# Conversions of weights spread differently over the attention, and the output weights of the first layer split two steps ahead

## The chip, the cores and the metric

The kernel runs on one core of a Trainium2 chip. The metric is the device time of one execution in microseconds (us), as the median of several runs. TensorE (PE) multiplies, VectorE (DVE), ScalarE (ACT) and GpSimd (POOL) work element by element, SyncE (SP) issues most of the transfers. Each engine takes its instructions in the order in which the program has them.

## The reference

Attention with a sigmoid in place of the softmax, then two dense layers with different activations; everything in float32.

```python
# q, k, v: (4 batches, 12 heads, 448 rows, 64)
scores = q @ k.T / sqrt(64) - log(448)
x = sigmoid(scores) @ v              # reordered to (1792, 768)
h = x @ w_in1;  x = silu(h) @ w_out1                  # 768 -> 2048 -> 768
h = x @ w_in2
g = (a0 + a1*h + a2*h**2 + a3*h**3) / (1 + |b0|*|h| + |b1|*h**2 + 1e-6)
out = g @ w_out2
```

The inputs q, k, v arrive as float32; the four weight matrices arrive as float64 bit patterns, that is as pairs of 32-bit words.

## The kernel before

**Precision.** TensorE multiplies in a format of fewer bits (fp32r). Each operand is split into a rounded high part (a copy on ACT) and a remainder (a subtraction on DVE, or on POOL in layer 2); a product is three matmuls: high by high, high by low, low by high.

**Conversions.** There are 64 weight tiles of 128x768: 16 of W_in and 16 of W_out for each of the two layers. `conv()` (L159 to L178) turns one from float64 bits into float32: one ACT instruction (L169, absolute value) and four DVE instructions (L170 to L175) on a tile that a transfer of 768 KB has put into one of two stage buffers (`stg`). `conv_outs()` then lets SP store the result (384 KB, to `w0i`, `w0o`, `w1i` or `w1o` in DRAM) and behind it load the float64 tile that is two conversions further on, into the stage buffer just read. So a conversion waits for the load that the conversion two before it has issued.

**Attention.** A loop over n = 0 to 47 (`for n in range(2 * NPT)`), two iterations for each pair of heads, four for each two pairs. An iteration issues: score matmuls of one or two units (`attn_QK`, L298, into `pair` tiles of PSUM, of which there are three), in odd iterations the transposes of a later pair of heads (`attn_T`, L272 and L275, into a `pair` tile too), the sigmoid of each unit (`attn_S`, ACT, L313, which frees the `pair` tile), the products with V of the units of the iteration before (`attn_AV`, L322, into `hb0` for even pairs of heads and `hb1` for odd ones), in every fourth iteration (n = 0, 4, ..., 44) the copies `attn_E` of both finished `hb` tiles out of PSUM (DVE, L335 or L338), then the split of the transposed tile (`attn_C`, ACT L281, DVE L283). From n = 21 on operands of layer 1 are made beside this; at n = 40 SP loads four tiles `wf` of converted W_in (L495), and at n = 43 ACT begins to split them (L355, and sums on DVE). Last in an iteration stands `conv()`, in those that the tuple `CONVS` lists; its store and the next load follow at the beginning of the next iteration. `CONVS` holds 19 iterations here: 2, the pairs (4, 5), (8, 9) to (24, 25), and 29, 33, 37, 42, 44, 46.

**Layer 1, first half.** x @ w_in1 in 16 groups (p1 to p7, seven block products for eight); 13 of the groups hold one conversion each. After `silu` the tiles `gd` go to DRAM.

**Layer 1, second half.** `second(n)` for n = 0 to 63 (L610 to L620): 18 matmuls with one tile pair `woH`, `woL` (split from `wos`, which ACT loads, L598) and one tile `gx` (split from `f`, which ACT loads from `gd`, L583). The order of the steps around n = 2, with the last pieces of the first half (`c21`, `both`, `c12`), is written out by hand. In loop n the split of the W_out tile is that of n + 1, the split of `gd` that of n + 2; the load of W_out n + 5 stands right behind the split that frees its buffer. The remaining conversions are spread by `conv_by(n)`: one in four steps up to n = 16, then evenly up to n = 52. Behind every 16 steps `results1` copies six results out of PSUM.

**Layer 2** follows with its own splits on POOL; the change does not touch it.

Of the kernel before, what the change touches and what calls it, by code (L numbers as in the profile page):

```python
# [41 lines left out]
def attention_moe_moe(ctx: ExitStack, tc: tile.TileContext, q, k, v, w_in1, w_out1, w_in2, w_out2, a, b2, out):  # L42
# [10 lines left out]
    KF = DFF // P  # L53
# [65 lines left out]
    def coefficients_abs():  # L119
        nc.scalar.activation(absb, ab[:, 4:6], AF.Abs)  # L120
# [223 lines left out]
    def split(src, x, eng=None):  # L344
        nc.scalar.copy(x[:, 0, :], src)
        (eng or nc.vector).tensor_tensor(out=x[:, 1, :], in0=src, in1=x[:, 0, :].bitcast(F32), op=ALU.subtract)

    def split2(src, h, lo, eng=None):
        nc.scalar.copy(h, src)  # L349
        (eng or nc.vector).tensor_tensor(out=lo, in0=src, in1=h.bitcast(F32), op=ALU.subtract)  # L350
# [148 lines left out]
    def silu(t, src, g, hi_f, second):  # L499
        nc.scalar.activation(t, src, AF.Silu)  # L500
        nc.sync.dma_start(out=gd[g % HF + hi_f * HF][2 * (g // HF) + second], in_=t)
        f448.put(t)
# [61 lines left out]
    def c12(g):  # L564
        silu(sums[g, "r"], sums[g, "r"], g, 0, 1)

    def c21(g):
        silu(f448.get(), bank("a", g), g, 1, 0)
# [16 lines left out]
    def split_gd(n):  # L585
        if n < B * KF:
            t = gq.pop(n)
            gx[n] = hl.get()
            split(t, gx[n])
            f448.put(t)  # L590
# [4 lines left out]
    def load_wo1(c):  # L595
        if c < KF:
            wo_in[c] = wos.get()
            nc.scalar.dma_start(out=wo_in[c], in_=wd[0][c]["o"])  # L598

    def split_wo1(c):  # L600
        if c < KF:
            t = wo_in.pop(c)
            split2(t, woH[c], woL[c])
            wos.put(t)
# [200 lines left out]
    with tc.manual_schedule():  # L805
# [24 lines left out]

        first_ops = operands0()
        NOPS = 7 * HK
        CONVS = (2, *(n for n in range(4, 28) if n % 4 < 2), 29, 33, 37, 42, 44, 46)
        waiting = []
        for n in range(2 * NPT):
            e, part = n // 4 * 2, n % 4
# [47 lines left out]
            if n == 12:  # L884
                coefficients_abs()
            if n in CONVS:
                conv()
# [136 lines left out]
        split_gd(2)  # L1024
        load_g(4)
        load_g(5)
        split_gd(3)
        NL1 = B * KF
        more = x_all.rearrange("p a b -> p (a b)").bitcast(I32).rearrange("p (e t) -> p e t", t=2)
        stage.put(more)  # L1030
# [8 lines left out]
        for n in range(2, NL1):  # L1039
            load_g(n + 4)  # L1040
            second(n)
            split_gd(n + 2)
            if n + 1 < KF:
                split_wo1(n + 1)
                load_wo1(n + 5)
            if n == 2:
                c21(last)
                both(last, "r", "c")
                c12(last)
            if n == KF - 1:  # L1050
                wos_s.close()
                l2_p = ctx.enter_context(tc.tile_pool(name="l2a", bufs=1, side="right", reuse_waits="tile"))
                hx.put(*fixed("hx", KD, [P, 2, BK], F32R, l2_p))
                wi_f.extend(fixed("wif", 4, [P, DM], F32, l2_p))
            if n % KF == KF - 1:
                results1(n // KF)
            conv_to(conv_by(n))
            m = n - (NL1 - KF)
            if m == 4:
                assert done["conv"] == len(order)  # L1060
            if m == 1:
                whr.put(w0[:2], w0[2:])
                for c in range(4):
                    load_w2("i", c)
            if m == 5:
                for d in range(HK):
                    load_x(0, d)
            if 7 <= m < 7 + KD:
                split_x(0, m - 7)
                if m - 7 < HK:  # L1070
                    load_x(0, m - 7 + HK)
            if m in (KF - 6, KF - 4):
                split_w("i", (m - KF + 6) // 2)
# [67 lines left out]
```

## Time and profile before

| | us |
|---|---|
| median of 3 runs | 1088.09 (1085.32 to 1091.08) |
| the profiled execution | 1086.84 |
| its span, first to last instruction | 1085.0 |
| PE busy | 1072.8 (99%) |
| DVE busy | 867.4 (80%) |
| ACT busy | 620.5 (57%) |
| POOL busy | 343.0 (32%) |

The attention runs from the beginning to 171.7 us, the first half of layer 1 to about 383, its second half to about 612, layer 2 to the end. The granted clock of TensorE is 0.999 on average. PE is the engine with the least idle time, so the time changes by what PE waits, and a change on another engine counts where PE comes to wait for it or no longer does. A matmul of 448 columns starts 0.20 us after the one before it when nothing holds it, although each is listed as 0.36 long: matmuls overlap, so what a stall costs is read from one start to the next.

### The profile page before, as it was taken

The page shows a single profiled execution, that of the slowest core. Times are in us where ns is not written, and L with a number is a line of the kernel's source. Part 1 is how long each engine was busy: PE and PEld are TensorE (multiplying, and loading weights), DVE is VectorE, ACT ScalarE, POOL GpSimd, SP SyncE. Part 2 cuts the span into 40 slices and gives each one's busy share as a digit, 9 for nine tenths or more (in the row PEclk, how much of TensorE's full clock was granted, in tenths as well). Part 3 has the DMA queues.
Part 4 walks back from the last instruction along what each step waited for, and adds up shares of the span by engine and source line. Part 5 has one row for each costly group of instructions (what it writes and reads, how often), then busy time and mean ns, then how long its engine had stood idle before and what let it go on. Part 6 is the DMA issues. An engine that isn't in the chain of part 4 may idle for free.

```text
span 1085.0 us, 15860 instructions
## 1 busy us (share of the span) xinstructions
PE 1072.8 (99%) x5822; PEld 913.9 (84%) x5822; DVE 867.4 (80%) x1030; ACT 620.5 (57%) x1023; POOL 343.0 (32%) x246
## 2 busy tenths in 40 slices
PE   9999999999999999999999999999999999999997
PEld 6555557999999988999999888889999888889997
DVE  4779877888977656887974397888999988888996
ACT  6678886656655534433333265556666655566664
POOL 2122210000000000000001175665777656657774
PEclk9999999999999999999999999999999999999999
DMA  8999877778576866998994470001011100101001
GB/s 211 275 292 269 248 228 245 252 247 275 172 251 221 281 222 218 335 347 303 358 329 160 175 284 1 23 22 50 9 30 31 44 1 1 32 14 59 1 1 44
DMA packets 102685, 177.96 MB, mean 164 GB/s; under 512 B 9168, under 2 KB 76752, under 8 KB 102608
## 3 DMA queue, kind: packets, MB, share of 16 engines
q1 hardware_dynamic: 90320, 155.38, 44.3%
q10 hardware_dynamic: 12224, 21.57, 6.2%
q8 instruction: 46, 0.75, 0.3%
q14 instruction: 31, 0.25, 0.1%
q0 software_dynamic: 64, 0.00, 0.0%
HBM read 123.31 MB, written 53.61 MB: 163 GB/s over the span
## 4 chain that ended last, share of the span: by engine, by line
PE 90%; DMA 3%; DVE 3%; ACT 2%; issue 1%; ACTq 1%; SPq 0%; POOL 0%; DVEq 0%; POOLq 0%
PE acc L748 14%; PE acc L481 13%; PE acc L751 7%; PE hb L677 7%; PE hb L678 7%; PE hb L679 7%; PE hb L481 5%; PE hb L322 5%; PE pair L298 5%; PE acc L619 5%; PE acc L617 5%; PE acc L618 5%; DMA stg<-in_moe_w_in_dram 2%; PE hb L619 1%; PE hb L617 1%; PE hb L618 1%
## 5 line engine op out<-in xcount | busy, mean ns | idle before, releaser
L350 POOL TENSOR_TENSOR w<-wif,w 128x768 fp32r<-128x768 f32 x33 | 61.2, 1855 | 444.0 <-DMA xio<-xs 438.1
L313 ACT ACTIVATE f<-pair,nls 128x896 f32<-128x896 f32 x84 | 80.6, 1007 | 21.9 <-PE pair L298 21.8
L705 DVE RECIPROCAL stg<-stg 128x512 f32<-128x512 f32 (+1 forms) x28 | 84.9, 3033 | 0.0
L692 ACT ACTIVATE stg<-hb,absb 128x512 f32<-128x512 f32 (+1 forms) x44 | 28.0, 636 | 99.0 <-PE hb L679 98.9
L169 ACT ACTIVATE bits<-stg 128x768 f32<-128x768 f32 x54 | 48.8, 904 | 54.2 <-DMA stg<-in_moe_w_in_dram 23.7
L322 PE MATMUL hb<-f,vs 128*64 128x448 f32 (+1 forms) x384 | 73.9, 554 | 0.0
L481 PE MATMUL acc<-xb,wr 128*128 128x448 f32 x315 | 67.7, 366 | 0.0
L350 POOL TENSOR_TENSOR wh<-wif,wh 128x768 fp32r<-128x768 f32 x31 | 57.3, 1850 | 27.5 <-ACT wh L349 25.6
L481 PEld LDWEIGHTS acc<-xb,wr 128*128 128x128 f32 x315 | 59.1, 188 | 5.3 <-issue 0.7
L748 PE MATMUL acc<-w,hx 128*128 128x512 f32 x174 | 61.4, 393 | 0.0
L618 PE MATMUL acc<-xa_all,woH 128*128 128x448 f32 x168 | 61.4, 365 | 0.0
L619 PE MATMUL acc<-xa_all,woL 128*128 128x448 f32 x168 | 61.4, 365 | 0.0
L617 PE MATMUL acc<-xa_all,woH 128*128 128x448 f32 x168 | 61.3, 365 | 0.0
L350 POOL TENSOR_TENSOR wh<-wof,wh 128x768 fp32r<-128x768 f32 x32 | 59.2, 1849 | 5.1 <-ACT wh L349 4.9
L748 PE MATMUL acc<-wh,hx 128*128 128x512 f32 x171 | 60.3, 393 | 0.0
L350 POOL TENSOR_TENSOR w<-wof,w 128x768 fp32r<-128x768 f32 x32 | 59.2, 1849 | 0.4 <-ACT w L349 0.2
L748 PE MATMUL acc<-wh,hy 128*128 128x512 f32 x165 | 58.9, 398 | 0.4 <-POOL hy L715 0.4
L748 PE MATMUL acc<-w,hy 128*128 128x512 f32 x162 | 57.3, 396 | 0.0
L170 DVE TENSOR_SCALAR bits<-bits 128x768 f32<-128x768 f32 x64 | 38.4, 599 | 21.8 <-ACT bits L169 21.1
L298 PEld LDWEIGHTS pair<-xa_all 64*128 64x128 f32 x384 | 34.3, 188 | 23.8 <-issue 11.3
L172 DVE SCALAR_TENSOR_TENSOR bits<-stg,bits 128x768 int32<-128x768 int32 x54 | 52.5, 972 | 1.9
L175 DVE SCALAR_TENSOR_TENSOR bits<-stg,bits 128x768 int32<-128x768 int32 x54 | 51.7, 958 | 1.9
(237 smaller groups left out, 3297.8 us busy)
## 6 DMA issues: line engine op xcount, KB each, us to landing
stg<-in_moe_w_in_dram SPq DMA_DIRECT2D x27, 768.0 KB, 7.4
stg<-in_moe_w_out_dram SPq DMA_DIRECT2D x27, 768.0 KB, 6.4
gd<-f SPq DMA_DIRECT2D x64, 224.0 KB, 3.2
f<-gd ACTq DMA_DIRECT2D x64, 224.0 KB, 4.8
wf<-w0i SPq DMA_DIRECT2D x32, 384.0 KB, 3.7
w0i<-bits SPq DMA_DIRECT2D x16, 384.0 KB, 4.1
w0o<-bits SPq DMA_DIRECT2D x16, 384.0 KB, 4.2
wos<-w0o ACTq DMA_DIRECT2D x16, 384.0 KB, 4.4
```

The costliest lines, as they stand in the source:

```text
L298: nc.tensor.matmul(p[:, j, :S], K[rows[j], a_, c * P : (c + 1) * P], Q[rows[j], b_, :], start=(n == 0), stop=(n == len(turns) - 1),)
L313: nc.scalar.activation(t, p[:, :, :S], AF.Sigmoid, bias=nls, scale=QKSCALE)
L322: nc.tensor.matmul(hb[i_ % 2][j * D : (j + 1) * D, :S], vs[i_][part, j, c * D : (c + 1) * D], t[part, j], start=(c == 0), stop=(c == LAST),)
L350: (eng or nc.vector).tensor_tensor(out=lo, in0=src, in1=h.bitcast(F32), op=ALU.subtract)
L481: nc.tensor.matmul(o, w_[:, w], x[:, i_, :], start=first and kk == 0 and n_ == 0, stop=kk == HK - 1 and n_ == 2, skip_group_check=not first,)
L617: nc.tensor.matmul(o, woH[c][:, w], x[:, 0, :], start=(c == 0), stop=False)
L618: nc.tensor.matmul(o, woH[c][:, w], x[:, 1, :], start=False, stop=False)
L619: nc.tensor.matmul(o, woL[c][:, w], x[:, 0, :], start=False, stop=(c == KF - 1))
L677: nc.tensor.matmul(o, wh[:, w], x[:, 0, :wd_], start=first, stop=False)
L678: nc.tensor.matmul(o, wh[:, w], x[:, 1, :wd_], start=False, stop=False)
L705: nc.vector.reciprocal(t0, t1)
L748: nc.tensor.matmul(acc[t][:, :BK], a_, w_[:, :BK], start=first, stop=last)
```

## The change

Three edits. The tuple `CONVS` has 18 iterations instead of 19: 10 instead of 13 up to n = 27, and 8 instead of 6 after it, 40, 42, 43, 45 and 46 among them. The 64 conversions stay; as the later ones are counted from what is done, all later conversions move by one place and `conv_by` has one more to spread over n = 17 to 52. `split_gd(3)` moves from ahead of the loop to n = 2. In the loop, W_out is split two steps ahead, its load stands in front of the split and ahead of the split of `gd`, and at n = 2 the last pieces of the first half come before the splits.

```diff
@@ attention
-        CONVS = (2, *(n for n in range(4, 28) if n % 4 < 2), 29, 33, 37, 42, 44, 46)
+        CONVS = (2, 6, 8, 10, 14, 16, 18, 22, 24, 26, 30, 34, 38, 40, 42, 43, 45, 46)
@@ layer 1, second half
         split_gd(2)
         load_g(4)
         load_g(5)
-        split_gd(3)
...
         for n in range(2, NL1):
             load_g(n + 4)
             second(n)
-            split_gd(n + 2)
-            if n + 1 < KF:
-                split_wo1(n + 1)
-                load_wo1(n + 5)
             if n == 2:
                 c21(last)
                 both(last, "r", "c")
                 c12(last)
+                split_wo1(3)
+                split_gd(3)
+            if n + 2 < KF:
+                load_wo1(n + 5)
+                split_wo1(n + 2)
+            split_gd(n + 2)
```

**DVE in iterations 43 and 44 of the attention.** `pair_276` is the last transposed tile, `sf` and `wf` belong to layer 1's weights, `bits` and `stg` to a conversion, `hb_274` and `hb_275` are `hb0` and `hb1`. Before:

```order
173 L283 TENSOR_TENSOR xa_all<-pair_276,xa_all 128x512
174 L283 TENSOR_TENSOR qx<-pair_276,qx 128x448
175 L367 TENSOR_TENSOR sf_246<-wf_1_243 128x384
176 L364 TENSOR_TENSOR sf_246<-sf_246,wf_0_242 128x384
177 L338 COPY xio<-hb_274 128x448
178 L338 COPY xio<-hb_275 128x448
179 L360 TENSOR_TENSOR wr_1850<-wf_0_242,wr_1849 128x768
180 L170 TENSOR_SCALAR bits_66<-bits_66 128x768
```

The same place after the change:

```order
165 L283 TENSOR_TENSOR xa_all<-pair_276,xa_all 128x512
166 L283 TENSOR_TENSOR qx<-pair_276,qx 128x448
167 L367 TENSOR_TENSOR sf_246<-wf_1_243 128x384
168 L364 TENSOR_TENSOR sf_246<-sf_246,wf_0_242 128x384
169 L170 TENSOR_SCALAR bits_64<-bits_64 128x768
170 L171 TENSOR_SCALAR bits_64<-bits_64 128x768
171 L172 SCALAR_TENSOR_TENSOR bits_64<-stg_63,bits_64 128x768
172 L175 SCALAR_TENSOR_TENSOR bits_64<-stg_63,bits_64 128x768
173 L338 COPY xio<-hb_274 128x448
174 L338 COPY xio<-hb_275 128x448
```

The conversion of n = 43 stands in front of the copies out of `hb0` and `hb1`; before, the next conversion came behind them.

**SP at n = 40 and behind it.** `vs` are loads of V, `wf` the loads of layer 1's first weights, `w0i` and `w0o` stores of converted tiles, `stg` loads for conversions, `xs` stores of attention results. Before:

```order
160 L201 DMA vs_1745<-in_v_dram 64x2x256
161 L495 DMA wf_0_242<-w0i_143 128x768
162 L495 DMA wf_1_243<-w0i_159 128x768
163 L495 DMA wf_0_244<-w0i_145 128x768
164 L495 DMA wf_1_245<-w0i_161 128x768
165 L155 DMA w0o_144<-bits_65 128x768
166 L143 DMA stg_62<-in_moe_w_out_dram 128x1536
```

The same place after the change:

```order
154 L201 DMA vs_1745<-in_v_dram 64x2x256
155 L495 DMA wf_0_242<-w0i_143 128x768
156 L495 DMA wf_1_243<-w0i_159 128x768
157 L495 DMA wf_0_244<-w0i_145 128x768
158 L495 DMA wf_1_245<-w0i_161 128x768
159 L155 DMA w0i_171<-bits_65 128x768
160 L139 DMA stg_63<-in_moe_w_in_dram 128x6x256
161 L155 DMA w0i_157<-bits_66 128x768
162 L143 DMA stg_62<-in_moe_w_out_dram 128x1536
```

Row 159 is now the store of the conversion of n = 40 (before, that of n = 42), and row 160 the load into `stg_63`, which the conversion of n = 43 reads.

**ACT in the second half of layer 1.** `wos` are loaded W_out tiles, `woH` their high parts, `f<-gd` loads and `xa` high parts of `gd`. Before, two steps (n = 4 and 5):

```order
432 L583 DMA f<-gd_0_111 128x448
433 L345 CAST xa_215<-f 128x448
434 L349 CAST woH_3702<-wos_3503 128x768
435 L598 DMA wos_3503<-w0o_162 128x768
436 L583 DMA f<-gd_0_115 128x448
437 L345 CAST xa_216<-f 128x448
438 L349 CAST woH_3704<-wos_3504 128x768
439 L598 DMA wos_3504<-w0o_164 128x768
```

After the change, two steps (n = 3 and 4):

```order
428 L583 DMA f<-gd_0_107 128x448
429 L598 DMA wos_3495<-w0o_160 128x768
430 L349 CAST woH_3695<-wos_3496 128x768
431 L345 CAST xa_all<-f 128x448
432 L583 DMA f<-gd_0_111 128x448
433 L598 DMA wos_3496<-w0o_162 128x768
434 L349 CAST woH_3697<-wos_3497 128x768
435 L345 CAST xa_215<-f 128x448
```

Before, the load into a `wos` buffer stands right behind the copy from that buffer; now a whole step lies between the two.

## Rows read from the trace of the kernel before

**Rows 1.** The page: engines over the span, and TensorE's granted clock in 40 slices.

```profile
PE 1072.8 (99%) x5822; PEld 913.9 (84%) x5822; DVE 867.4 (80%) x1030; ACT 620.5 (57%) x1023; POOL 343.0 (32%) x246
...
PEclk9999999999999999999999999999999999999999
```

**Rows 2.** Waits of PE: who waited for whom, total us, times, longest us.

```profile
PE pair L272 <- ACT f L313: 1.7, 3, 0.6
PE hb L619 <- DVE woL L350: 1.7, 2, 1.0
```

**Rows 3.** Timeline of PE, attention, n = 7: start, us, what, idle before.

```profile
32.69 0.78 PE L298 MATMUL pair<-xa_all 64*128 64x448 f32 x6
34.01 0.63 PE L272 MATMUL pair<-ident,km 128*128 128x128 f32 x4 [0.55 <-ACT f L313]
```

**Rows 4.** Timeline of ACT, attention: conversions of n = 5 and 9.

```profile
32.06 0.90 ACT L169 ACTIVATE bits<-stg 128x768 f32<-128x768 f32 x1 [3.48 <-DMA stg<-in_moe_w_in_dram]
...
46.18 0.90 ACT L169 ACTIVATE bits<-stg 128x768 f32<-128x768 f32 x1 [2.55 <-DMA stg<-in_moe_w_in_dram]
```

**Rows 5.** Timeline of SP, attention: the load for the conversion of n = 9.

```profile
37.33 0.39 SPq L139 DMA_DIRECT2D stg<-in_moe_w_in_dram  x1
```

**Rows 6.** Timeline, layer 1, second half, PE and ACT at n = 7 and 11.

```profile
402.01 0.37 PE L618 MATMUL hb<-xa,woH 128*128 128x448 f32 x1
...
403.43 0.47 PE L619 MATMUL hb<-xa,woL 128*128 128x448 f32 x1 [1.05 <-DVE woL L350]
...
404.25 0.57 ACT L345 CAST xa_all<-f 128x448 fp32r<-128x448 f32 x1 [4.27 <-DVE woL L350]
...
417.92 0.36 PE L618 MATMUL hb<-xa_all,woH 128*128 128x448 f32 x1
...
418.89 0.47 PE L619 MATMUL hb<-xa_all,woL 128*128 128x448 f32 x1 [0.61 <-DVE woL L350]
```

**Rows 7.** Timeline of PE: first matmuls of second(2) and second(3).

```profile
383.57 0.36 PE L617 MATMUL hb<-xa_all,woH 128*128 128x448 f32 x1
...
387.22 0.36 PE L617 MATMUL hb<-xa_all,woH 128*128 128x448 f32 x1
```

**Rows 8.** Timeline of ACT in layer 1: results1 at n = 31.

```profile
492.42 0.53 ACT L625 COPY f<-acc 128x448 f32<-128x448 f32 x1 [8.84 <-PE acc L619]
```

**Rows 9.** Timeline of ACT, n = 42 (a conversion) and 43 (split of wf).

```profile
154.90 0.89 ACT L169 ACTIVATE bits<-stg 128x768 f32<-128x768 f32 x1
...
158.60 0.84 ACT L355 CAST wr<-wf 128x768 fp32r<-128x768 f32 x1
```

**Rows 10.** Timeline of DVE, n = 40 to 44.

```profile
149.91 0.62 DVE L364 TENSOR_TENSOR xk<-xk,xk 128x448 f32<-128x448 f32 x1
...
158.00 0.96 DVE L175 SCALAR_TENSOR_TENSOR bits<-stg,bits 128x768 int32<-128x768 int32 x1
...
160.59 0.56 DVE L364 TENSOR_TENSOR sf<-sf,wf 128x384 f32<-128x384 f32 x1
161.68 1.16 DVE L338 COPY xio<-hb 128x448 f32<-128x448 f32 x2 [0.53 <-PE hb L322]
```

**Rows 11.** Timeline of PE, n = 45: second score unit, then the V products.

```profile
162.28 0.78 PE L298 MATMUL pair<-qx,xa_all 64*128 64x448 f32 x6
162.99 1.72 PE L322 MATMUL hb<-f,vs 128*64 128x448 f32 x8
```

**Rows 12.** Timeline of SP: the four loads of wf.

```profile
152.43 2.01 SPq L495 DMA_DIRECT2D wf<-w0i  x4
```

**Rows 13.** DMA issues near 154.1: KB each, median us to landing.

```profile
wf<-w0i SPq DMA_DIRECT2D x1, 384.0 KB, 5.9
```

**Rows 14.** DMA issues, 117 to 119 us: load and store of one conversion.

```profile
stg<-in_moe_w_in_dram SPq DMA_DIRECT2D x1, 768.0 KB, 6.0
w0i<-bits SPq DMA_DIRECT2D x1, 384.0 KB, 2.9
```

**Rows 15.** Timeline of PE: the first score matmuls of the kernel.

```profile
7.37 2.61 PE L298 MATMUL pair<-xa_all 64*128 64x448 f32 x12
```

## The prediction

> **What bounds the kernel now.** I read the page first. PE is busy for 99% of the span and its granted clock stands at 9 tenths or more in every slice [rows 1], so nothing that is merely moved between the other engines changes the time; only a wait of PE does. Next I read the waits of PE. Two groups lie where the change works: three waits in the attention, 1.7 us together, ended by a sigmoid on ACT, and two in the second half of layer 1, 1.7 us together, ended by the split of W_out on DVE [rows 2]. Then I followed each back in the timelines.
>
> In the attention, the six score matmuls of n = 7 that start at 32.69 are done in 0.71, so the transposes were due at 33.40; they start at 34.01 [rows 3]. They wait for the `pair` tile that the sigmoid frees, and ACT was late because it stood for 3.48 in front of the conversion of n = 5, whose stage buffer was still loading; the conversion of n = 9 stands for 2.55 in the same way [rows 4]. The loop behind it: conversion at 32.06, next load into that buffer issued at 37.33, landed for 46.18 [rows 4, 5]. That is 14.1 us, where four iterations of PE without a stall take 13.5 (14.1 less the 0.6 of the stall). Conversions in pairs, two in four iterations, each pair feeding the next, thus lose 0.6 per turn, until the loads become faster.
>
> In layer 1 the second matmul of n = 7 starts at 402.01 and the third, which reads `woL`, at 403.43; at n = 11 the pair is 417.92 and 418.89 [rows 6]. Behind the first of these ACT is idle for 4.27 until DVE has split `woL` [rows 6]: the load that stands right behind the copy on ACT may not overwrite the buffer before DVE has read it, and everything on ACT stands behind that load. Steps with a conversion on top then take longer than the 3.65 us that PE needs (383.57 to 387.22 [rows 7]).
>
> **The change part by part.**
>
> *Attention, first part: gain 1.9.* Ten conversions instead of thirteen. The two stage buffers alternate, so a conversion depends on the one two before it in the list: 6 feeds 10, 8 feeds 14, 10 feeds 16, 14 feeds 18. The distances are now 4, 6, 6 and 4 iterations, and the distance of four is always followed by a longer one, so lateness cannot add up as it does before, where all are four. At a distance of four the load is 0.6 late (14.1 against 13.5). ACT stood 2.55 to 3.48 when PE lost 0.6, so a wait of 0.6 on ACT stays within what PE can bear, 2 us or more. I take all three stalls as gone: 3 x (34.01 - 33.40) = 1.8, with the others read alike 1.9. Bounds: 0 and 1.9. If the cover were gone, the old 0.6 would come back at each distance of four, 1.8 again.
>
> *Layer 1, second half: gain 2.0.* The two stalls cost 403.43 - 402.01 - 0.20 = 1.22 and 418.89 - 417.92 - 0.20 = 0.77. With the load a whole step behind the split that frees its buffer, ACT no longer stands for DVE, and a conversion has two steps of 3.65 in place of one to be made up. At the start it is tight: `both` needs p3, which ends at 383.57; then come `both` (0.6), `c12` (0.5), the copy of W_out 3 (0.8) and the two DVE splits (1.0 and 0.6), one after another 383.8 + 3.5 = 387.3, and PE wants them at 387.22 [rows 7] and, for the low parts, 0.2 and 0.4 later. I price this at 0.1, bounds 0 and 1. Sum 2.0 - 0.1 = 1.9.
>
> *One conversion more in the second half of layer 1: nothing.* ACT waits there for PE, not the reverse: at n = 31 it had been idle for 8.84 when PE finished [rows 8]. One conversion more (0.9 on ACT, 3.1 on DVE) fits under that. Without the cover it would cost at most these 4.
>
> *Attention, end: a loss, 6.1.* Conversions at n = 42 and 43 in a row are new, and n = 43 is the iteration ahead of the copies out of `hb0` and `hb1` (n = 44). DVE keeps its order, so the four DVE instructions of the conversion now stand in front of these copies. The first V product of n = 45 overwrites `hb0`: now it starts at 162.99 [rows 11], and the first of the two copies is done at 161.68 + 0.58 = 162.3 [rows 10]. That leaves 0.7 of slack.
>
> The conversion of n = 43 can start on ACT at 158.60 + 0.84 = 159.44 [rows 9] if its tile has landed. From its start on ACT to its last DVE instruction a conversion takes 4.06: 154.90 to 158.00 + 0.96 [rows 9, 10]. With DVE busy until 160.59 + 0.56 = 161.15 and 3.1 of DVE work, the copy is done no earlier than 161.15 + 3.1 + 0.6 = 164.9: 1.9 lost even without any wait for a transfer.
>
> But its tile is late. It is loaded by the conversion of n = 40, two before it in the list but only three iterations (10.1 us) earlier. DVE reaches that one behind the subtraction at 149.91 + 0.62 [rows 10] and is done at 153.7. On SP its store and load stand behind the four loads of `wf`, issued until 154.44 [rows 12], so the load is issued at about 154.9. When does it land? Three rows give three answers. A load in light traffic took 6.0 [rows 14]: 160.9. One in the dense part took 8.85 (37.33 to 46.18): 163.8. And the last `wf` load, issued at 154.1 just ahead of it, took 5.9 [rows 13], that is until 160.0; store and load behind it take, as in rows 14, the 3.9 between their landings (117.9 + 2.9 = 120.8 and 118.7 + 6.0 = 124.7) and some 1.2 for the store: 165.1. I take 164.4, between the last two, because the loads of `wf` lie right in front.
>
> Then the conversion ends at 164.4 + 4.06 = 168.5, the copy at 169.1, and the V product that was due at 162.99 starts there: 6.1 lost. The sigmoids of n = 44 stand behind the conversion on ACT too, but are done at 164.4 + 0.9 + 1.9 = 167.2, inside the same wait. What follows has slack again: the conversion of n = 46 gets its load some 5 us after 168.5 and PE, shifted by 6.1, asks for it no sooner. Bounds: 1.9 (no wait for the transfer) and 8.7 (landing at 167).
>
> The Trainium skill (DMA: Bandwidth & Descriptors, "Queues, rings and completion order") says that each DMA engine takes the descriptors of one queue in ring order. By it the load cannot pass the `wf` loads, and the sum would go by 165.1 (a loss of 6.8) and not by 160.9 (2.6); rows 13 are in line with it, the last of four loads having been the slowest, which one row alone does not prove.
>
> **Sum.** -1.9 - 1.9 + 6.1 = +2.3. The profiled execution took 1086.84 (span 1085.0), so 1089.1; it lies 1.25 below the median of the runs, 1088.09, which gives 1090.4. I forecast 1089.9, in the middle: a hair slower, and within what a measurement of this kernel can tell from no change (about 0.5%, 5.4 us).
>
> **The rivals.**
>
> *The load lands early.* If it comes by 161, as in light traffic, the loss at the end is 1.9 to 2.7, and the sum -1.9 to -1.1: 1087. For it: 154 to 160 has fewer loads of q, k and v than the middle of the attention. Against it: the 1.5 MB of `wf` right ahead.
>
> *TensorE's clock falls in the new stall.* This is the case on the slower side. PE would stand from 163.0 until the sigmoid of n = 44 frees its `pair` tile at 166.2, run six matmuls, and stand again until 169.1. No row shows such a gap; the granted clock stayed up through every wait of before, the longest near 1 us in rows 2. What lower speed costs is seen at the start, where twelve score matmuls took 2.61 [rows 15] against twice 0.78 in rows 3, 1.1 more. Two such groups remain in the attention, with the V products between: 2.2 at least, so +4.5 (1092), and with a landing at 167 +7 (1094.6). It decides from a landing of about 165 on.
>
> The Trainium skill (TensorE: Matmul & The Clock Gate, "What's actually happening") states that idleness throttles the array to half its clock and activity releases it. No run here shows it yet; it speaks for this rival.
>
> *The gains do not come.* A distance of four iterations still stalls PE, or the start of the second half (387.2) loses what the two stalls gave back: then the sum is +4 to +6, 1092 to 1094.
>
> *The end does not stall*, because the copies or the load are not where I put them: -3.8, 1084.3.
>
> **How the numbers follow.** Forecast (stall of 4 to 8 at the end, both gains) 0.46; load early 0.20; clock falls 0.16; gains do not come 0.10; no stall 0.08. The range takes the early landing at its lower end, less the spread of the runs, and the falling clock with a late landing at its upper: 1085.5 to 1095.5. The likeliest case alone is 1088 to 1092. Slower by over 0.5% (above 1093.5): most of the clock case 0.09, part of the gains case 0.04, late landing without the clock 0.04, in all 0.17. Faster by over 0.5% (below 1082.7) needs more than all gains together: 0.04 for what I have not seen. The rest, 0.79, is the same.
>
> **What would show it.** Right: PE's waits no longer name L313 in front of L272 in the first 65 us, nor `woL`; a new wait of about 6 us in front of L322 near 163 (less 1.9 for the earlier gains, so near 161), ended by the DVE copy L338, and ahead of it ACT idle in front of L169 for some 5 us, ended by a transfer. Wrong: no wait at L322 there, or one of 2 us (landing early); a granted clock under 1.00 near 165 (clock); waits of PE at L617 to L619 around n = 3; waits before L272 that stay.

## The result and the profile after

| | before | after |
|---|---|---|
| median | 1088.09 (15 runs) | 1098.95 (15 runs, 1090.15 to 1101.68) |
| ratio of the means to before, 95% | | 1.0083 (1.0061 to 1.0105) |
| profiled execution, span | 1086.84, 1085.0 | 1095.82, 1094.0 |
| mean granted clock | 0.999 | 0.995 |

The change makes the kernel slower: by 10.9 us in the medians, by 9 in the means (the ratio). 1089.9 was forecast, with 1095.5 as the upper end: the prediction was wrong. The profiled execution is 3 us below the median of its runs; why they lie so far apart turned out to be a part of the answer.

The page of after, beside [rows 1]:

```profile
PE 1078.2 (99%) x5822; PEld 914.6 (84%) x5822; DVE 862.8 (79%) x1030; ACT 621.9 (57%) x1023; POOL 341.3 (31%) x246
...
PEclk9999998999999999999999999999999999999999
```

PE is busy for 5.4 us longer though it runs the same 5822 matmuls, and one slice, the seventh, has a lower clock. The waits of PE after, beside [rows 2]:

```profile
PE pair L298 <- ACT f L313: 4.8, 1, 4.8
PE hb L322 <- DVE xio L338: 1.5, 1, 1.5
```

Both old groups are gone, and two waits of one place stand in their stead. That place in PE's timeline of after, beside [rows 11], and the first matmul of layer 1:

```profile
159.59 0.87 PE L298 MATMUL pair<-xa_all 64*128 64x448 f32 x6
165.24 1.36 PE L298 MATMUL pair<-qx,xa_all 64*128 64x448 f32 x6 [4.78 <-ACT f L313]
168.06 3.25 PE L322 MATMUL hb<-f,vs 128*64 128x448 f32 x8 [1.45 <-DVE xio L338]
...
178.74 1.50 PE L481 MATMUL acc<-xb,wr 128*128 128x448 f32 x6
```

Six score matmuls take 0.71 from start to start [rows 11], so the V product was due at 159.59 + 2 x 0.71 = 161.01, which is 1.98 sooner than the 162.99 of [rows 11]; it started at 168.06, 7.05 late. ACT and DVE of after, beside [rows 9, 10], show why:

```profile
163.40 0.89 ACT L169 ACTIVATE bits<-stg 128x768 f32<-128x768 f32 x1 [5.93 <-DMA stg<-in_moe_w_in_dram]
164.19 3.69 ACT L313 ACTIVATE f<-pair,nls 128x896 f32<-128x896 f32 x4
```

```profile
164.32 0.56 DVE L170 TENSOR_SCALAR bits<-bits 128x768 f32<-128x768 f32 x1 [5.15 <-ACT bits L169]
...
167.39 1.15 DVE L338 COPY xio<-hb 128x448 f32<-128x448 f32 x2
```

ACT stands before the conversion of n = 43 until its tile has landed, the sigmoids stand behind it, and DVE's copies stand behind the conversion's four instructions. Layer 1 then begins at 178.74 instead of 171.71, 7.03 late: 7.05 less 1.98 is 5.07, and 1.96 more were lost between 168 and 178. The windows of after say where, and show one thing more (columns: stretch, its length, PE busy with its matmuls, granted clock, DMA share, GB/s):

```profile
155.00:185.00 30.00, 23.77 (x133) 0.89 0.77 252
200.00:370.00 170.00, 170.00 (x824) 1.00 0.69 234
435.00:605.00 170.00, 170.00 (x840) 1.00 0.85 297
```

The same stretches of before:

```profile
200.00:370.00 170.00, 170.00 (x840) 1.00 0.72 242
435.00:605.00 170.00, 170.00 (x840) 1.00 0.83 291
```

The clock is down to half for about 2 x 0.11 x 30 = 6.6 us of the first (the expectations below say 6.8). And in the first half of layer 1, at a granted clock of 1.00 and with no wait, PE did 824 matmuls in 170 us where it did 840: one every 206.5 ns in place of 202.5 (the expectations below say 206.7 and 202.7, from single starts, and call the longer one the slow rhythm). These are means: single starts lie 199 to 207 ns apart in the shorter rhythm, and 206 or 207 in the longer one. The first half takes 204.70 from its first L481 to its first L617, and took 200.75. These 3.95 are the third part of the loss, and the prediction has no term for them.

### The profile page after: what moved, and what is told of

The parts are those of the page before. It is cut to its first block, busy times and chain, and to the rows that moved or that the text cites. A ratio compares the mean times of both kernels' runs of the same rounds, so it can differ in the third digit from the quotient of the medians.

```text
span 1094.0 us, 15861 instructions
## 1 busy us (share of the span) xinstructions
PE 1078.2 (99%) x5822; PEld 914.6 (84%) x5822; DVE 862.8 (79%) x1030; ACT 621.9 (57%) x1023; POOL 341.3 (31%) x246
## 4 chain that ended last, share of the span: by engine, by line
PE 92%; DVE 2%; DMA 2%; ACT 2%; issue 1%; POOL 0%; SPq 0%; ACTq 0%; DVEq 0%; POOLq 0%
PE acc L748 14%; PE acc L481 14%; PE acc L751 7%; PE hb L677 7%; PE hb L678 7%; PE hb L679 7%; PE acc L618 5%; PE acc L619 5%; PE acc L617 5%; PE hb L481 5%; PE hb L322 4%; PE pair L298 4%; PE hb L618 2%; PE hb L619 2%; PE hb L617 2%; DMA stg<-in_moe_w_in_dram 2%
## 5 line engine op out<-in xcount | busy, mean ns | idle before, releaser
L313 ACT ACTIVATE f<-pair,nls 128x896 f32<-128x896 f32 x84 | 80.5, 1005 | 35.6 <-PE pair L298 35.5
L481 PE MATMUL acc<-xb,wr 128*128 128x448 f32 x315 | 68.9, 369 | 0.0
L481 PEld LDWEIGHTS acc<-xb,wr 128*128 128x128 f32 x315 | 59.1, 188 | 6.6 <-issue 0.7
L617 PE MATMUL acc<-xa_all,woH 128*128 128x448 f32 x168 | 61.4, 366 | 0.0
L619 PE MATMUL acc<-xa_all,woL 128*128 128x448 f32 x168 | 61.4, 365 | 0.0
```

The source lines that it names most:

```text
L313: nc.scalar.activation(t, p[:, :, :S], AF.Sigmoid, bias=nls, scale=QKSCALE)
L481: nc.tensor.matmul(o, w_[:, w], x[:, i_, :], start=first and kk == 0 and n_ == 0, stop=kk == HK - 1 and n_ == 2, skip_group_check=not first,)
L617: nc.tensor.matmul(o, woH[c][:, w], x[:, 0, :], start=(c == 0), stop=False)
L619: nc.tensor.matmul(o, woL[c][:, w], x[:, 0, :], start=False, stop=(c == KF - 1))
```

## The experiments

The order is by what they answer. In all the traces the two halves of layer 1 take one of a few values, so one table serves them all. "First half" runs from the first L481 to the first L617, "second half" from the first matmul of n = 4 to the first L677, each without a listed wait unless one is named (the 18.2 to 18.6 us between them are in neither); the pause is PE's waits between 157 and 171. "Clock" is the mean granted clock.

| trace | pause | clock, 155 to 185 | first half | second half | that execution |
|---|---|---|---|---|---|
| before | 0 | 1.00 | 200.75 | 221.07, waits of [rows 2] in it | 1086.84 |
| after | 4.78 + 1.45 | 0.89 | 204.70 | 218.88 | 1095.82 |
| after, second execution | 3.90 + 1.33 | 0.89 | 204.70 | 218.88 | 1094.85 |
| after, third execution | 4.14 + 1.33 | 0.83 | 200.74 | 218.88 | 1090.77 |
| after, fourth execution | 4.20 + 1.32 | 0.83 | 200.75 | 218.88 | 1090.90 |
| n=43 to n=36 | 0 | 1.00 | 200.75 | 218.88 | 1083.35 |
| n=43 to n=36, again | 0 | 1.00 | 202.54, a wait of 1.4 in it | 218.88 | 1084.49 |
| layer-1 part alone | 0 | 1.00 | 200.75 | 223.20 | 1090.57 |
| conversions alone | 4.49 + 1.32 | 0.89 | 204.69 | 219.90, a wait of 0.2 in it | 1096.85 |
| small transposes in the gap | 1.33 + 1.33 | 0.89 | 200.78 | 218.88 | 1090.34 |
| matmuls in the gap | 0.98 + 1.94 | 0.89 | 204.70 | 218.88 | 1096.02 |
| tile early | 1.74 | 1.00 | 202.38, a wait of 1.2 in it | 223.20 | 1090.48 |
| one split late | 4.43 + 1.33 | 0.89 | 204.69 | 223.20 | 1100.06 |
| one split late, real wait | 4.85 + 1.32 | 0.83 | 204.69 | 221.08, waits in it | 1098.92 |
| pause alone, long | 7.20 | 0.83 | 204.69 | 223.20 | 1102.04 |
| pause alone, short | 2.60 | 0.94 | 204.70 | 218.88 | 1092.39 |
| wait before layer 1 | 5.09 + 1.32 | 0.89 | 200.75 | 223.20 | 1097.97 |

A half at 206.5 ns costs 3.95 (204.70 - 200.75) or 4.32 (223.20 - 218.88).

### Is the stall the conversion at n = 43?

```diff
-        CONVS = (2, 6, ..., 26, 30, 34, 38, 40, 42, 43, 45, 46)
+        CONVS = (2, 6, ..., 26, 30, 34, 36, 38, 40, 42, 45, 46)
```

> The changed kernel with the conversion of n = 43 moved to n = 36, nothing else. Theory A (the loss is the conversion at n = 43: its tile is late, the copies out of hb0 stand behind it, PE idles 4.8 + 1.5 us at n = 45, the granted clock falls to one half for 6.8 us, and TensorE then issues a matmul every 206.7 ns instead of 202.7 ns up to 398 us): all three parts go, no wait of PE near 160, granted clock 1.00, 202.7 ns in layer 1, span about 1085.0 - 2.0 - 2.0 = 1081, ratio to the kernel before 0.994 to 0.998. Rival B (the slower matmuls come from the order in layer 1 or from other conversions of the tuple): 206.7 ns stays, span 1085 or more. Rival C (late convs at 40, 42, 45, 46 suffice): a wait of 1 us or more of PE at n = 41 to 47.

Measured 1083.42 (ratio 0.9959, 0.9936 to 0.9983). By PE's timeline the V product of n = 45 starts behind the scores with no wait:

```profile
161.08 0.78 PE L298 MATMUL pair<-qx,xa_all 64*128 64x448 f32 x6
161.78 1.72 PE L322 MATMUL hb<-f,vs 128*64 128x448 f32 x8
```

So the one conversion carries the whole loss, the clock and the longer rhythm with it, and with it moved the change beats the kernel before by 4 us: the two gains forecast, in this trace 1.2 up to layer 1 (170.50 against 171.71) and 2.2 in the second half. Moving it takes away both the late tile and its place ahead of the copies; the early tile below separates the two. The same kernel in a further set of executions:

> The kernel with the conversion at n=43 moved to n=36 once more, with more executions and another chip as it falls. Theory A (a pause of TensorE at the attention's end is what starts layer 1 in the slow rhythm): without a pause most executions lie within 1 us of the lowest, 1082 to 1084, few at 1088 and hardly any above, median 1083.4 and a ratio to the kernel before of about 0.996. Rival B (the slow rhythm comes by itself, as often without a pause as with one; eight of ten at 1083.4 were luck): the executions spread evenly from 1082 to 1091 as they spread from 1090 to 1100 with the pause, median 1086 to 1087.

1083.72 (0.9967, 0.9952 to 0.9981), 11 of its 12 executions from 1082.95 to 1084.49. Of the 22 of both, 19 lie below 1084.5. Windows of its trace:

```profile
155.00:185.00 30.00, 30.00 (x180) 1.00 0.80 274
200.00:370.00 170.00, 170.00 (x841) 1.00 0.72 246
```

### The two parts of the change apart

The kernel before with the layer-1 edits only:

> The kernel before with only the edits of layer 1's second half (W_out two steps ahead, split_gd(3) moved), CONVS as before. Theory A: the two waits at L619 go and nothing else changes: span 1085.0 - 2.0 = 1083, ratio 0.997 to 0.999. Rival B (these edits are what slows TensorE in layer 1): 206.7 ns a matmul somewhere in 170 to 400 us and a span of 1087 or more.

1085.82 (0.9975, 0.9952 to 0.9999): a gain of about 2 as forecast. Its trace is of the slowest execution of ten, 1090.57, and has what rival B named, a span over 1087 and the longer rhythm, though only from 389 on: it runs the second half at 206.5 ns, with no fall of the clock and no listed wait ahead of it since 41 us; so the rhythm is no after-effect of the clock alone. The median speaks against B, the trace does not. Early in the attention, where the trace of before has three waits of 0.6 [rows 2], this execution of the same attention has one of 2.43, and the clock at half for 3.4 us behind it:

```profile
35.36 0.63 PE L272 MATMUL pair<-ident,km 128*128 128x128 f32 x4 [2.43 <-ACT f L313]
...
36.90:40.40 3.50, 3.50 (x14) 0.51 1.11 323
```

The kernel before with the new `CONVS` only:

> The kernel before with only the new CONVS, layer 1's second half as before. Theory A: the whole loss is here, and the two waits at L619 (2.0 us) are still to be seen: span 1094.0 + 2.0 = 1096 in a run like the profiled one of the changed kernel, ratio 1.008 to 1.013. Rival B (the loss is in layer 1's edits): span 1085 or less.

1095.87 (1.0060, 1.0042 to 1.0078), with the least spread of all, 1092.79 to 1096.85. Here the old order of layer 1 leaves a short wait in the second half. There, in PE's timeline, the longer rhythm ends that had lasted since 179:

```profile
428.88 0.47 PE L619 MATMUL hb<-xa_all,woL 128*128 128x448 f32 x1 [0.24 <-DVE woL L350]
```

### Four executions of the changed kernel

> The changed kernel itself, one more look. Theory A (the rhythm of 206.7 ns, kept for a shorter or a longer stretch of layer 1, makes the difference between its executions): a profiled execution of about 1096 has the slow rhythm in one half of layer 1 as the first one had, one of 1099 to 1101 in all of layer 1, one of 1090 to 1092 in hardly any of it; the stall near 160 us (about 7 us) and the fall of the clock behind it (about 2 us) are the same in each. Rival B (executions differ by the stall or by the length at the lower clock): the waits near 160 us or the stretch at half clock differ by the same microseconds.

> The changed kernel itself, a further look, with the same expectations: the stall near 160 us and the fall of the clock are the same in each execution, and the time goes with the number of matmuls that TensorE starts every 206.7 ns in place of 202.7 (theory A), or with the stall and the clock (rival B).

> The changed kernel once more, timed on one chip beside the next two, since its executions lie anywhere from 1090 to 1102. Theory A and rival B both expect 1096 to 1099 here; it is the kernel that the next one is compared with.

1094.85, 1090.77, and 1093.99 as a median of 10 (1.0057, 1.0033 to 1.0082), below the 1096 to 1099 expected of it. Windows of the third execution:

```profile
155.00:185.00 30.00, 24.53 (x131) 0.83 0.77 254
200.00:370.00 170.00, 170.00 (x840) 1.00 0.72 245
435.00:605.00 170.00, 170.00 (x841) 1.00 0.85 297
```

The stall is there and the clock fell for longer, yet it is 5 us faster than the first execution, because neither half is at 206.5 ns. So an execution of this kernel takes 1090.8 with neither half slow, 4 to 5 more with the first (1094.85 and 1095.82), and by the sum 1099.1 with both, of which no trace was taken. Its 27 timed executions lie so: 8 at 1090.2 to 1092.6, 8 at 1093.5 to 1096.4, 11 at 1098.4 to 1101.7. The median of 1098.95 is the uppermost group, the 1093.99 of another chip the middle.

### Does work in the gap keep the clock?

After n = 45's first score unit, 38 transposes of 64x64 more:

```diff
-            ready = [(u, attn_QK(*u)) for u in units]
+            ready = [(u, attn_QK(*u)) for u in units[:1]]
+            if n == 45:
+                for _ in range(38):
+                    nc.tensor.transpose(ready[0][1][:, 0, S : S + D], ident[:D, :], ident[:D, :D])
+            ready += [(u, attn_QK(*u)) for u in units[1:]]
```

> The changed kernel with 38 transposes without use on TensorE between the two score units of n = 45, into unused columns of the first unit's pair tile; they need some 2.3 to 4.7 us, inside the gap of 4.8. The waits for the conversion of n = 43 stay. Theory A (the clock falls because TensorE idles, and the slower matmuls follow from the fall): granted clock stays 1.00, matmuls at 202.7 ns, span 1094.0 - 2.0 (half clock) - 4.0 (slower matmuls) = 1088, ratio 1.001 to 1.005. Rival B (the slower matmuls come from the wait itself, not from the clock): clock 1.00 but 206.7 ns stays: span 1092. Rival C (38 transposes are not enough activity): all as in the changed kernel, 1094 to 1098.

1093.76 (1.0046, 1.0009 to 1.0082). They filled 2.55 of the gap, by PE's timeline:

```profile
160.42 2.55 PE L852 MATMUL pair<-ident 64*128 64x64 f32 x38
164.31 1.49 PE L298 MATMUL pair<-qx,xa_all 64*128 64x448 f32 x6 [1.33 <-ACT f L313]
167.12 3.26 PE L322 MATMUL hb<-f,vs 128*64 128x448 f32 x8 [1.33 <-DVE xio L338]
```

The clock fell all the same, to half for about 6.6 us (0.89 over 30 us, as in the changed kernel), as rival C had it; this execution has neither half in the longer rhythm, others of the ten reach 1100.5.

Then the first score unit of n = 45 computed seven times, 36 matmuls of full size more:

```diff
...
-        for n, (i_, (a_, b_)) in enumerate(turns):
+        for n, (i_, (a_, b_)) in list(enumerate(turns)) * times:   # 7 for this unit
```

> The changed kernel with the first score unit of n=45 computed seven times over, each time from the start into the same tile (36 matmuls of 448 columns more, some 4.3 us of them, all inside the stretch in which TensorE waits for the late tile). The stall keeps its length: the V product still starts about 168 us. Theory C1 (the clock fell because TensorE had too little to do, and 38 transposes of 64 columns were too little as well): with matmuls as dense as the scores themselves the granted clock stays at 1.00 or falls for a shorter stretch, which gives back up to 2.0 us, and the lowest executions come to about 1088 in place of 1090. Theory C2 (the start after the wait brings the lower clock whatever ran in the gap): half clock for 6.8 us again, lowest execution about 1090. For the slow rhythm of layer 1 (206.7 ns a matmul in place of 202.7): if it follows from the fall of the clock, layer 1 begins at 202.7 and the spread of the times is that of the kernel before; if it follows from the wait itself, about two of three executions are still slow.

1096.22 (1.0076, 1.0051 to 1.0102). PE's timeline in the stall:

```profile
159.47 4.53 PE L298 MATMUL pair<-xa_all 64*128 64x448 f32 x42
164.98 0.88 PE L298 MATMUL pair<-qx,xa_all 64*128 64x448 f32 x6 [0.98 <-ACT f L313]
167.79 3.25 PE L322 MATMUL hb<-f,vs 128*64 128x448 f32 x8 [1.94 <-DVE xio L338]
```

and its window:

```profile
155.00:185.00 30.00, 27.08 (x166) 0.89 0.74 254
```

C1 fell: two gaps of 1 and 2 us with 0.9 us of work between them brought the lower clock for as long as before. The rhythm of layer 1 was the longer one again, at a median like that of the changed kernel. Filling the gap is no cure.

### The tile early, the conversion where it is

```diff
-        CONVS = (..., 30, 34, 38, 40, 42, 43, 45, 46)
+        CONVS = (..., 30, 34, 36, 38, 42, 43, 45, 46)
```

> The changed kernel with the conversion of n=40 moved to n=38 and one of n=36 left out (…30, 34, 38, 40→ as …30, 34, 36, 38, 42, 43, 45, 46): the weight tile that the conversion at n=43 reads is then loaded after an earlier conversion, about 10 us sooner, and the conversion at n=43 stays where it is. Theory A (the stall near 160 us is the late tile, with VectorE's conversion standing ahead of the two copies to xio): the wait of ScalarE for the tile goes, the scores of n=45 are taken up without a wait, and what is left is VectorE's order alone, the conversion's four instructions ahead of the copies: some 1.9 us on the V product, and no fall of the clock, or a short one. Span about 1083.5, median 1085 to 1087 if layer 1 runs at one matmul every 202.7 ns, up to 8.5 more where it runs at 206.7. Rival B (the mere place of the conversion at n=43 among VectorE's instructions is what costs 7 us): the wait stays near 6 to 7 us and the clock falls as in the changed kernel, 1094 to 1100.

The tuple loses 40 and gains 36, so none of the 18 is left out. 1090.22 (1.0010, 0.9985 to 1.0035), 3 us above the 1087 that was the upper end without the longer rhythm. PE's wait:

```profile
162.66 1.72 PE L322 MATMUL hb<-f,vs 128*64 128x448 f32 x8 [1.74 <-DVE xio L338]
```

and its windows:

```profile
155.00:185.00 30.00, 28.26 (x169) 1.00 0.85 274
435.00:605.00 170.00, 170.00 (x825) 1.00 0.85 297
```

The mechanism is as stated: without the late tile only DVE's order is left, 1.74 for the 1.9 of the lower bound, and the clock stays at 1.00. But the executions spread from 1085 to 1094, and this one has its second half at 206.5 ns, with no fall of the clock before it. That the pause of 1.74 brought it there is not shown: the layer-1 part alone has the same second half without any pause near 160.

### Is it the pause?

The fastest kernel (n = 43 to n = 36) with the pause alone put back, by repeating one DVE copy in front of which nothing else moves:

```diff
-        nc.vector.tensor_copy(t[:, :S], hb[i % 2][:, :S])
+        for _ in range(13 if i == 20 else 1):      # 6 in the short one
+            nc.vector.tensor_copy(t[:, :S], hb[i % 2][:, :S])
```

> The kernel with the conversion at n=43 moved to n=36 (it ran at 1083.4, without a wait near 160 us), with VectorE's first copy to xio at n=44 made thirteen times instead of once (12 x 0.56 = 6.7 us), so that the V product due at 161.8 waits about 6 us. No tile is late and no conversion is moved: only TensorE's pause is put back. Theory A (a pause of TensorE at this place is what brings the lower clock, and with it or after it the slow rhythm, whatever made the pause): half clock for about 6.8 us behind it, + 6 + 2 = 8 us, lowest execution about 1090 and the median at 1094 to 1098, since layer 1 begins at 206.7 ns a matmul in more than half of the executions. Rival B (the slow rhythm comes from the late transfer or the other order of the conversions): 1083.4 + 8 = 1091 to 1092, with few executions above.

1100.13, five executions (1.0095, 1.0060 to 1.0130), above the 1094 to 1098 of theory A; PE's wait (lines behind L338 stand one number higher):

```profile
169.09 3.25 PE L322 MATMUL hb<-f,vs 128*64 128x448 f32 x8 [7.20 <-DVE xio L339]
```

and its windows:

```profile
155.00:185.00 30.00, 22.80 (x131) 0.83 0.60 210
200.00:370.00 170.00, 170.00 (x825) 1.00 0.67 231
435.00:605.00 170.00, 170.00 (x825) 1.00 0.86 301
```

> The kernel with the pause alone (conversion at n=43 moved to n=36, first copy to xio at n=44 repeated), with six copies in place of thirteen: 5 x 0.56 = 2.8 us more work on VectorE than without repeats, a pause of TensorE of about 3.3 us in place of 7.2. Theory A1 (the slow rhythm goes with the fall of the clock): if the granted clock does not fall behind a pause of 3.3 us, layer 1 begins at 202.7 ns a matmul and the median is about 1083.4 + 3.3 = 1086.7 to 1087.5; if it falls, 2 us more and the spread of the changed kernel, median 1091 to 1097. Theory A2 (the slow rhythm goes with the pause, not with the clock): 1088 to 1095 with the clock at 1.00 behind it.

1096.15, six executions (1.0064, 1.0032 to 1.0095). PE's wait:

```profile
165.00 2.62 PE L322 MATMUL hb<-f,vs 128*64 128x448 f32 x8 [2.60 <-DVE xio L339]
```

and its windows:

```profile
155.00:185.00 30.00, 27.40 (x163) 0.94 0.78 269
200.00:370.00 170.00, 170.00 (x824) 1.00 0.70 241
```

The long pause moved the start of layer 1 by 10.1 (180.59 against 170.50) and the median by 16.7; the short one by 4.8 (175.31) and 12.7. In both, 6.6 to 8 us more are lost than the pause and the clock explain. Nothing but the copies was added: a pause of PE at this place brings the longer rhythm, whatever made the pause. (The sets come from different chips, but the kernel before took 1087.0 to 1088.4 on each.) Without it 19 of 22 executions are at the lowest level; with it two of eleven are within 2.1 us of where pause and clock alone would put them (1092.07 against 1083.4 + 10.1 = 1093.5, and 1090.28 against 1088.2). The clock fell behind 2.6 us as well, so A1 and A2 could not be told apart here, nor by the early tile above: its clock stayed, but its first half was in the shorter rhythm.

### Is a further wait a cure?

In the changed kernel, tile 7 of W_out split a step later:

```diff
...
             split_gd(n + 2)
+            if n == 6:                  # and not at n == 5
+                split_wo1(7)
+                load_wo1(11)
```

> The changed kernel with one split of layer 1 made late again: tile 7 of W_out is split at the end of step 6 (as in the kernel before) and not in step 5, so that TensorE waits once, at n=7, about 1.7 us. Theory A (the rest of the loss is a rhythm of 206.7 ns a matmul in place of 202.7, taken up when TensorE sets off after a wait and kept while it runs without one): the wait costs 1.7 us but gives the rhythm a new start at about 413 us; where the stretch after it would have stayed slow the wait saves up to 200/4.. that is some 1,000 matmuls by 4 ns = 4 us, so that the executions near 1099 to 1101 become rarer and the median falls to about 1096 to 1097, with the lowest ones 1.7 us above those of the changed kernel. Rival B (the rhythm has nothing to do with the waits): the median rises by 1.7 us to about 1100.5.

1097.63 (1.0078, 1.0049 to 1.0106). No wait came of it: the split was done at 411.6, second(7) began at 413.0. So it says nothing on the wait; it is one more execution of the changed kernel, with both halves at 206.5 ns (824 matmuls in each of the two windows), and it took 1100.06.

With the same split made three times over there was a wait:

> The changed kernel with tile 7 of W_out split at the end of step 6 as before, and three times over (two more casts of 0.83 us and subtractions of 0.96 us in turn), since the split at the end of step 6 alone was done 1.5 us before it was wanted and made no wait. Its last subtraction should end some 3.8 us later, at about 415, while the first L617 or L619 of n=7 is due at about 413: one wait of TensorE of about 2 us. Theory A (a wait gives the rhythm a new start): where the first half of layer 1 ran at 206.7 ns, it runs at 202.7 behind this wait in most executions, as the wait of 0.24 us at 429 us did it in the kernel with the conversions alone; the executions near 1099 to 1101 vanish, the median falls from 1099 to 1096 or 1097, in spite of 2 us of wait. Rival B (waits and rhythm have nothing to do with each other): the median rises by 2 us to about 1100.5.

1097.29, four executions (1.0079, 1.0050 to 1.0108). The rhythm changes at the wait, by PE's timeline

```profile
415.22 0.47 PE L617 MATMUL hb<-xa,woH 128*128 128x448 f32 x1 [1.13 <-ACT woH L349]
...
416.21 0.47 PE L619 MATMUL hb<-xa,woL 128*128 128x448 f32 x1 [0.31 <-DVE woL L350]
```

and the windows ahead of it and behind it:

```profile
200.00:370.00 170.00, 170.00 (x824) 1.00 0.69 233
435.00:605.00 170.00, 170.00 (x841) 1.00 0.87 304
```

A expected that of the trace; four executions are too few to say more of the median than that it did not rise. Last, a wait just before layer 1, by making the last sigmoid twice:

```diff
-        nc.scalar.activation(t, p[:, :, :S], AF.Sigmoid, ...)
+        for _ in range(2 if (i, c) == (NPT - 2, LAST) else 1):
+            nc.scalar.activation(t, p[:, :, :S], AF.Sigmoid, ...)
```

> The changed kernel with the last Sigmoid of the attention (n=47, one instruction of 1.01 us) made twice, so that the last V product waits some 0.4 us at about 178 us, just before layer 1; the stall near 160 us and the fall of the clock behind it stay. Theory A (the slow rhythm of 206.7 ns is taken up behind the stall and carried into layer 1 for want of a further wait; a wait gives it a new start): layer 1 begins at 202.7 ns a matmul in the trace, executions near 1098 to 1102 become rare, and the median falls by 4 to 7 us against the changed kernel, to about 1091 to 1093, though the work and the stall are the same or more. Rival B (the rhythm is not bound to waits, or the wait is no new start for it): the median rises by 0.4 us.

1098.72, eight executions (1.0079, 1.0048 to 1.0110), beside 1093.99 for the changed kernel on the same chip: a miss. PE's wait (lines behind L313 stand one number higher):

```profile
180.06 0.98 PE L323 MATMUL hb<-f,vs 64*64 64x448 f32 x8 [0.55 <-ACT f L314]
```

and its windows:

```profile
200.00:370.00 170.00, 170.00 (x841) 1.00 0.69 238
435.00:605.00 170.00, 170.00 (x824) 1.00 0.85 297
```

The first half began at 202.5 ns behind the wait, as expected, but the second ran at 206.5 without any wait before it. A wait can end the longer rhythm; it does not keep it away.

## Why the prediction was wrong

*Attention, first part, -1.9:* right in kind. The three waits on L313 are gone, and the work before n = 45 is 1.98 earlier. That is the difference of two traces, and executions differ there: the first score unit of n = 45 starts at 161.57 in before and at 163.32 in the layer-1 part alone, and from 158.8 to 161.5, 159.9 on average, in the fifteen traces with the new `CONVS`. A gain of about 2 is shown, its tenths are not.

*Layer 1, second half, -1.9:* right. Both L619 waits are gone; from n = 4 to layer 2 it takes 218.88 in place of 221.07, 2.2 less, and the tight start of n = 3 cost no listed wait. But it is the place where the rhythm of the second half is settled. In all fifteen traces with the new order DVE finishes the last operand of n = 3 (L346) within 0.05 us of PE's first matmul of that step, so near that any hold is too short to be listed. In seven of the fifteen the rhythm changes right there, from shorter to longer in three (4.32 each) and back in four; in the two traces with the old order it does not. In the layer-1 part alone, where it turned longer:

```profile
388.22 0.62 DVE L346 TENSOR_TENSOR xa_all<-f,xa_all 128x448 fp32r<-128x448 f32 x1
...
388.80 0.37 PE L617 MATMUL hb<-xa_all,woH 128*128 128x448 f32 x1
```

That the late operand turns it is not shown, since no run gave this operand more time. The conversion more was hidden as stated: ACT still waits at L625 for PE, up to 19.2 at a time.

*Attention, end, +6.1:* the mechanism as written, step by step: tile late, ACT standing for 5.93, DVE's copies behind the conversion, the V product late. Measured 7.05 in the first execution, and 6.2, 6.4 and 6.5 in the other three, reckoned alike. In the first, the tile landed at about 163.4; with the 1.98 of the first part added that is 165.3 on the clock of before, where I took 164.4. The answer by the place in the queue was the better one:

```profile
153.26 0.61 SPq L139 DMA_DIRECT2D stg<-in_moe_w_in_dram  x1
...
stg<-in_moe_w_in_dram SPq DMA_DIRECT2D x1, 768.0 KB, 10.1
```

issued at 153.26 behind the loads of `wf`, it took 10.1 (9.2 to 9.8 in the other three). The Trainium skill (DMA: Bandwidth & Descriptors, "Queues, rings and completion order") has each DMA engine take the descriptors of a queue in ring order, which is not yet the order of landing; the sum by that rule was 165.1, and this trace agrees within 0.2.

*The sum, +2.3,* is the step that failed. It took a stall to cost its length and let PE go on behind it as before. Two terms were missing. The first stood there as a rival, with a chance of 0.16: the clock. It fell to half for about 6.6 us, and cost 1.96 where 2.2 was priced; in the third and fourth executions, with 10.2 us at half, 2.7. That the price came out is in part luck, for the granted clock stands at 1.00 over [rows 15] (a window of before):

```profile
7.30:10.00 2.70, 2.70 (x14) 1.00 0.77 219
```

So that row shows slow matmuls but not the lower clock; what that does is seen in after, where eight V products take 3.25 in place of 1.72. The fall should have been the forecast: "no row shows such a gap" was the reason against it, and the longest wait of [rows 2], near 1 us, was no evidence on one of 6. Another execution of the same attention would have shown more: the wait of 2.43 in the layer-1 part alone, with the clock at half behind it. The Trainium skill (TensorE: Matmul & The Clock Gate, "What's actually happening") has idleness throttle the array and activity release it; the trace with the wait of 2.43 and every trace with a single wait of 2.6 or more agree, and in one with 1.74 the clock stayed. (The middle of 1089.1 and 1090.4 is 1089.8, not 1089.9.)

For the profiled execution the parts add up: -1.98 - 2.19 + 7.05 + 1.96 + 3.95 = 8.8, of the 9.0 between the spans. Without the second term the change costs +4.1: the fourth execution of after, which has stall and clock but no half at 206.5 ns, took 1090.90 against 1086.84. Its layer 1 starts 6.4 later (178.14 against 171.71) and takes 2.2 less in the second half; the rival "clock" had +4.5.

The second term was in no case of the prediction: the rhythm of layer 1, 0 to 8.3 by the execution, and 8 in the median of 1098.95 (less the 1090.9 of the fourth execution). What is shown: the two rhythms (840 and 824 matmuls in 170 us), that each half of layer 1 without a wait takes one of two times, that the changed kernel's executions fall into the groups that these make, and that a pause alone brings the longer one to a kernel which hardly ever has it. The first half was in it in 8 of 11 traces with a pause of over 2 us in all between 157 and 171 and no wait behind it, and in none of the 5 with less, the one with 2.43 at 33 us among them. Transfers do not tell the rhythms apart: the DMA share of the second half is 0.85 in the first execution of after, in the shorter one, and 0.85 with the tile early, in the longer one. What is not shown is the mechanism: what in a pause leads to it, what makes it begin or end at n = 3 in some traces and not in others, and whether the fall of the clock adds to it. That the spread of before (1085 to 1093) is of the same making fits, but its one trace has the shorter rhythm throughout.

*The rivals.* Load early, gains that do not come, and no stall at the end: none of them.

## What to carry to other kernels

A pause that is new on the engine that bounds the kernel costs more than its length: price the lower clock behind it as part of the forecast, and treat a pause of several us at full load as something to be moved away, not as a term to be set against small gains. Before spacing work evenly, look where in the engines' order the moved piece now stands: one conversion in front of two copies cost three times what the whole change gained, and moving that one made it a gain of 4 us. And where executions of one kernel fall into groups, take traces of several before explaining a difference.

## What was not expected of the hardware

- At a granted clock of 1.00 and with no wait, TensorE started the same 448-column matmuls every 202.5 or every 206.5 ns, for a hundred us and more on end (840 or 824 in 170 us).
- 42 score matmuls in a row in the gap, with waits of 0.98 and 1.94 after them, did not keep the clock up; 38 small transposes did not either. A single wait of 1.74 left it at 1.00.
